# Sliding-window attention and a two-layer FFN on one core: five blocks' attention first, casts on GpSimd in load order, two output banks in every tile, column sums late

## The chip, the core and the metric

The kernel runs on one core of a Trainium2 chip. A core has a matrix engine (PE, which multiplies a stationary 128x128 operand with a moving one and writes its results to PSUM), a vector engine (DVE), an activation engine (ACT), GpSimd (POOL) and a sync engine (SP), which here only issues transfers. Each engine works through its own list of instructions in order; they meet at semaphores. PSUM has eight banks of 128 x 512 float32. The time is device microseconds (us) from start to end of one execution.

## The reference

Eight batches of eight heads, 576 positions, 64 channels per head. Each position attends to the positions at most 32 away; the result, heads side by side, is a matrix x of 4608 x 512, which goes through an FFN with a squared relu.

```python
scores = scale * np.matmul(q, k.transpose(0, 1, 3, 2))      # scale = 1/8
scores = np.where(np.abs(pos[:, None] - pos[None, :]) <= 32, scores, -1e9)
attn = np.exp(scores - np.max(scores, axis=-1, keepdims=True))
attn = attn / (np.sum(attn, axis=-1, keepdims=True) + 1e-09)
x = heads side by side of np.matmul(attn, v)                # 4608 x 512
h = x @ w_in                                                # 512 -> 2048
g = s * np.maximum(h, 0.0) ** 2 + b                         # s, b scalars
out = g @ w_out                                             # 2048 -> 512
```

The scalars are moved out of the second product: out = s * (r*r @ w_out) + b * (column sums of w_out). The last term is one vector, CVEC, spread over 128 partitions; it has to be there before the first output row can be finished.

## The kernel before

The 4608 rows are 36 blocks of 128. Attention works block by block (`attend(j)`), the FFN by tiles (`TILES`: eight of one block, then fourteen of two).

**Attention of a block.** q and k are loaded as float32 and cast to bf16 (`cast_q`, `cast_k`, line 471 through the helper `move`), turned on PE (`k_turn`, `q_turn`; bank TP) and copied to SBUF as kqt. A load can come in rows of 2 KB, eight positions each (`rows8`), which needs `turn_rows8` (line 528, 16 small matmuls), or in 256-byte pieces, one per head and position, with `turn_plain` (line 542, four). Scores (line 582) go to two banks, SC. DVE masks them and takes the extreme (line 598), ACT exponentiates and sums (line 606), DVE takes the reciprocal (line 617), and eight scalings of 128x128 (line 472) make P: on any of three engines for the first `NDIV` = 4 blocks, on GpSimd for the rest. P is turned on PE in the bank PTP for the first `PDMA` = 4 blocks (line 640), by a DMA transpose from block 4 on (line 633), and lands as PTS. The product with v (line 662) goes to the bank AV, and DVE copies it to XT, the FFN's input. Block 0 is worked in two halves (`FINE`), its second half in the banks HT1 and OUTP. From block 4 on, v's copy `vo` with halves swapped is made too (`make_vo`).

**FFN of a tile.** The first product (line 752) fills HT banks of 512 columns: for a tile of one block, 16 matmuls of 128 columns each, four such groups, one per quarter i0 to i3 of w_in. ACT takes the relu (line 761), DVE squares it into GT (line 780). The second product (line 803) takes 16 matmuls of 512 columns per block, in four groups of four, one per quarter o0 to o3 of w_out, into OUTP, or OUTP and PTP in turn after the first `NSOLO` = 2 blocks. DVE adds CVEC and writes the output tile (line 812), SP stores it. The last three tiles may use four banks.

**Weights.** w_in and w_out come as eight quarters of 1 MB (`load_w`) through four staging slots, which lie in a part of GT that tile 4 is the first to need. Each quarter is cast in four pieces, w_in's on GpSimd, w_out's on ACT or GpSimd.

**Column sums.** `cvec` multiplies a matrix of ones with all of w_out, four groups of four 512-column matmuls in OUTP (line 688), then scales on DVE (line 694). Output groups that use OUTP come behind it.

**The order.** Nothing is scheduled at run time. `_Plan` collects all steps with their data, an assumed cost and a key, and works out each engine's list once, when the kernel is built: at every step the engine that can go first takes its ready step with the lowest key. Wherever the plan sees PE idle over 300 ns at the start, it puts in filler matmuls (`fill`, lines 395 and 398), into banks that hold nothing yet. `FIRST` is the order of the first loads on SP's queue; the number of bars in it is the number of blocks whose attention is written ahead of the first tile's FFN. Steps on one bank are bound to the order in which they are written.

## Time and profile before

| | |
|---|---|
| Time, median of 3 runs | 329.05 us (328.51 to 329.32) |
| The profiled execution: time, span | 328.95 us, 327.2 us |
| PE, DVE, ACT, GpSimd busy | 96%, 71%, 65%, 56% of the span |
| First product, line 752, into ht and tp | 115.4 + 33.2 us busy on PE |
| Second product, line 803, into outp and ptp | 72.2 + 61.6 us busy on PE |
| DMA | 61.75 MB, 189 GB/s; packets under 512 B: 163820 of 173949 |
| Weight quarter, issue to landing | 11.4 us (w_in), 11.7 us (w_out), queueing included |

Busy time of PE overlaps between neighbouring matmuls, so a group's length from start to start is shorter than the duration that a line of the timeline shows. In a timeline, a line gives the start, the length of the group, the engine, the source line, the operation, what is written and read, and in brackets the idle time before it with what ended it. In a table by stretches, each engine's busy time is followed by its number of instructions; the last three columns are the granted clock of PE, the busy share of DMA and its GB/s. SPq is the sync engine issuing a transfer. A line "x16" of the first product is one group of 16 matmuls.

### The profile page before, as it was taken

To read this page: it belongs to the slowest core of one execution; us is meant where nothing else is said; L and a number is where in the kernel's file an instruction comes from. 1 tells how busy PE (TensorE), PEld (TensorE's weight loads), DVE (VectorE), ACT (ScalarE), POOL (GpSimd) and SP (SyncE) were. 2 spreads that over 40 slices of the span, in tenths; PEclk is the share of its full clock that TensorE was granted. 3 is DMA by queue.
4 is the path that set the end of the run, shared out by engine and by line. 5 is a ranking of instruction groups with operands and counts; after the bars stand their busy time and mean duration, and the time that the engine had idled before them with its cause. 6 is when DMAs were issued, how large, how long until landed. Compare 5 with 4: busy or idle time off the path is not lost.

```text
span 327.2 us, 10194 instructions
## 1 busy us (share of the span) xinstructions
PE 312.7 (96%) x3821; PEld 212.5 (65%) x3821; DVE 232.8 (71%) x988; ACT 214.0 (65%) x753; POOL 182.5 (56%) x394
## 2 busy tenths in 40 slices
PE   6675999999999999999999999999999999999996
PEld 4554776567767666766666666666666666666664
DVE  3459988879888878878787777777777677442432
ACT  3563896668769887867766666667777876533330
POOL 2537474897657988766655668486667453300000
PEclk9999999999999999999999999999999999999999
DMA  5999999999999999999999999999994332120011
GB/s 125 310 326 330 355 232 195 236 235 210 202 213 205 213 215 200 238 216 216 237 244 181 209 224 239 210 190 238 210 228 117 91 78 73 47 64 34 32 59 71
DMA packets 173949, 61.75 MB, mean 189 GB/s; under 512 B 163820, under 2 KB 164076, under 8 KB 173900
## 3 DMA queue, kind: packets, MB, share of 16 engines
q1 hardware_dynamic: 173612, 61.10, 88.3%
q8 instruction: 30, 0.49, 0.6%
q14 instruction: 19, 0.16, 0.2%
q10 hardware_dynamic: 288, 0.00, 0.0%
HBM read 36.70 MB, written 9.44 MB: 141 GB/s over the span
## 4 chain that ended last, share of the span: by engine, by line
PE 81%; DMA 7%; DVE 5%; SPq 4%; ACT 2%; issue 0%
PE ht L752 27%; PE outp L803 17%; PE ptp L803 16%; PE tp L752 9%; DMA q<-in_q_dram 4%; PE av L662 4%; PE sc L582 3%; DMA v<-in_v_dram 3%; PE sc L803 2%; ACT p L606 2%; PE av L803 2%; SPq L421 2%; DVE gt L780 1%; SPq L447 1%; SPq L450 1%; DVE kqn L471 1%
## 5 line engine op out<-in xcount | busy, mean ns | idle before, releaser
L472 POOL TENSOR_SCALAR p<-p,rc 128x128 bf16<-128x128 bf16 x257 | 101.8, 415 | 52.9 <-DVE rc L617 52.9
L606 ACT ACTIVATE p<-ss,mx 128x128 bf16<-128x128 f32 x288 | 111.8, 391 | 23.2 <-DVE mx L598 21.4
L752 PE MATMUL ht<-xt,win 128*128 128x256 bf16 (+1 forms) x1152 | 115.4, 249 | 0.6 <-POOL win L471 0.4
L752 PEld LDWEIGHTS ht<-xt,win 128*128 128x128 bf16 x1152 | 91.0, 98 | 23.7 <-POOL win L471 0.6
L780 DVE TENSOR_TENSOR gt<-r 128x512 bf16<-128x512 bf16 x144 | 68.5, 477 | 43.0 <-ACT r L761 42.2
L761 ACT ACTIVATE r<-ht 128x512 bf16<-128x512 f32 x112 | 66.3, 593 | 43.9 <-PE ht L752 40.3
L598 DVE CUSTOM_DVE_ANT_0 ss<-sc,mask 128x128 f32<-128x128 f32 x288 | 66.1, 282 | 18.0 <-PE sc L582 17.9
L803 PE MATMUL outp<-wout,gt 128*128 128x512 bf16 (+1 forms) x288 | 72.2, 374 | 0.0
L803 PE MATMUL ptp<-wout,gt 128*128 128x512 bf16 x240 | 61.6, 380 | 0.0
L606 ACT ACTIVATION_READ_ACCUMULATOR p<-ss,mx 128x1 f32 x288 | 54.4, 189 | 0.0
L471 POOL CAST ve<-v 128x512 bf16<-128x512 f32 x37 | 24.9, 672 | 29.1 <-PE av L662 16.6
L803 PEld LDWEIGHTS outp<-wout,gt 128*128 128x128 bf16 x288 | 26.1, 98 | 18.2
L803 PEld LDWEIGHTS ptp<-wout,gt 128*128 128x128 bf16 x240 | 22.3, 98 | 17.2
L752 PE MATMUL tp<-xt,win 128*128 128x256 bf16 x256 | 33.2, 273 | 0.0
L761 ACT ACTIVATE r<-tp 128x512 bf16<-128x512 f32 x32 | 18.9, 591 | 21.8 <-PE tp L752 20.6
L752 PEld LDWEIGHTS tp<-xt,win 128*128 128x128 bf16 x256 | 24.6, 98 | 8.8
L471 DVE CAST vo<-v 64x512 bf16<-64x512 f32 x54 | 27.1, 503 | 2.6 <-DMA v<-in_v_dram 1.8
L471 DVE CAST xt<-av 128x512 bf16<-128x512 f32 x35 | 24.0, 687 | 3.6 <-PE av L662 2.8
L598 DVE DVE_READ_ACCUMULATOR2_ANT mx<- 128x1 f32 x288 | 23.2, 81 | 0.0
L471 POOL CAST kqn<-q 128x512 bf16<-128x512 f32 x30 | 20.2, 672 | 2.9 <-DMA q<-in_q_dram 2.7
L471 POOL CAST kqn<-k 128x512 bf16<-128x512 f32 x31 | 19.0, 614 | 4.6 <-DMA k<-in_k_dram 4.5
L582 PEld LDWEIGHTS sc<-kqt 64*64 64x64 bf16 x864 | 12.1, 108 | 9.4 <-issue 6.5
(68 smaller groups left out, 228.4 us busy)
## 6 DMA issues: line engine op xcount, KB each, us to landing
out_dram<-outs SPq DMA_DIRECT2D x35, 256.0 KB, 3.4
q<-in_q_dram SPq DMA_DIRECT2D x32, 256.0 KB, 4.8
k<-in_k_dram SPq DMA_DIRECT2D x28, 256.0 KB, 4.8
v<-in_v_dram SPq DMA_DIRECT2D x28, 256.0 KB, 4.9
gt<-in_moe_w_in_dram SPq DMA_DIRECT2D x4, 1024.0 KB, 11.4
gt<-in_moe_w_out_dram SPq DMA_DIRECT2D x4, 1024.0 KB, 11.7
k<-in_k_dram SPq DMA_DIRECT2D x8, 192.0 KB, 3.8
v<-in_v_dram SPq DMA_DIRECT2D x8, 192.0 KB, 3.8
```

The costliest lines, as they stand in the source:

```text
L421: lastload[0] = add("sp", lambda e: [e.dma_start(w32, src)], 500, -LEAD - 900, writes=[("W32", s_, g) for g in range(4)], dsem=f"dw{s_}", ...
L447: return [e.dma_start(dst[r:r + n, :], src[b, :, s0:s0 + n, :].rearrange("h (c r) d -> c h (r d)", r=8)) for (b, s0, r, n) in pcs]
L471: return e.tensor_copy(dst, src)
L472: return e.tensor_scalar(dst, src, scale, 1.0, ALU.mult, ALU.mult)
L582: r = e.matmul(SC[hh][64 * u:64 * u + 64, pr, x0:x1], lhsT=KQT[kb][64 * hh:64 * hh + 64, NPAIR + pr, 64 * u:64 * u + 64], rhs=KQT[kt][64 * ...
L598: lambda e, ss=ss, x=x, y=y, pr=pr, hh=hh: e.tensor_tensor_reduce(out=SS[ss][:, x, :], in0=SC[hh][:, pr, :], in1=MASK[kind][:, :], scale=- ...
L606: lambda e, ss=ss, x=x, y=y: e.activation(P[pb][:, y, :], SS[ss][:, x, :], AF.Exp, bias=MX[mb][:, y:y + 1], scale=-1.0, accum_out=SM[mb][: ...
L662: r = e.matmul(avp[64 * hh:64 * hh + 64, pr, 64 * u:64 * u + 64], lhsT=vt[k0:k1, d0:d0 + 64], rhs=PTS[ptb][k0:k1, 2 * pr + hh, 64 * u:64 * ...
L752: r = e.matmul(hbank[:, nt * f:nt * f + nt], lhsT=WIN[:, kc, 128 * ft:128 * ft + 128], rhs=XT[:, kc, x0:x0 + nt], start=(kc == 0), stop=(k ...
L761: return e.activation(R1[rb][:, :], hbank[:, :], AF.Relu, bias=0.0, scale=1.0)
L780: return e.tensor_tensor(d, r, r, ALU.mult)
L803: r = e.matmul(op_[:, 0:cn], lhsT=GT[:, g_, fc, :], rhs=WOUT[:, fc, c0:c0 + cn], start=(fc == 0), stop=(fc == 15))
```

## The change

- `FIRST`: q1, k2, v2 go ahead of i0; i0 and i1, i2 and i3, and all of o0 to o3 follow each other. Five bars instead of three.
- All weight casts are GpSimd's, and all q and k casts from q1 and k2 on. Casts of the first loads get keys in the order of `FIRST` (`ckey`).
- k0 and q4 are no longer loaded in rows of 2 KB but in 256-byte pieces (`KROWS`, `QROWS`).
- P is turned in AV's bank (for the second half of block 0 in PTP's, where its product with v goes too), so that PTP is free for the second product: `NSOLO` is gone, and OUTP and PTP take turns from the first tile on.
- The column sums are written behind the second product of tile 0. 16 matmuls with 32 columns of ones put four partial sums into four strips of 32 partitions of TP; ACT copies them as bf16 (CHI), DVE writes the remainder (CLO), and two matmuls with a matrix of 1/32 (PART) add the strips; DVE scales to CVEC.
- Three assumed DMA times are raised by 170 or 150.

```diff
-    FIRST = "k0 q0 k1 v0 v1 i0 q1 k2 v2 i1 i2 q2 k3 v3 i3 o0 q3 k4 v4 o1 o2 o3|||"
+    FIRST = "k0 q0 k1 v0 v1 q1 k2 v2 i0 i1 q2 k3 v3 i2 i3 q3 k4 v4 o0 o1 o2 o3|||||"
-    WSET = {"i": ("pool",), "o": ("act", "pool")}
+    WSET = {"i": ("pool",), "o": ("pool",)}
-    ROWS8, NDIV = 5, 4
+    CKEY = 200
+    QROWS, KROWS, NDIV = range(0, 4), range(1, 5), 4
...
     def CSET(j):
-        return ANY if j < 6 else ("pool",)
+        return ("act", "dve") if j < 1 else ("pool",)
...
+        place = {x: i for i, x in enumerate(FIRST.replace("|", " ").split())}
+        def ckey(what, j, key):
+            return -9000 + 10 * place[what + str(j)] if what + str(j) in place else key
...
-                              dtime=2680, behind=lastload[0], ndesc=512)
+                              dtime=2850, behind=lastload[0], ndesc=512)
...
-                ptp, pres, avp, ares = PTP, "PTP", AV, "AV"
+                avp, ares = AV, "AV"
                 if fine and part:
-                    ptp, pres = halves(HT[1]), ("HT", 1)
-                    avp, ares = OUTP[:, :].rearrange("p (a b) -> p a b", b=128), ("OUTP", 0)
+                    avp, ares = PTPF[:, :].rearrange("p (a b) -> p a b", b=128), "PTP"
+                ptp = halves(PTPF if fine and part else AVF)
...
         def cvec():
-            for c in range(4):
-                def fn(e, c=c):
-                    for fc in range(4 * c, 4 * c + 4):
-                        r = e.matmul(OUTP[:, :], lhsT=ONES[:, 0:128], rhs=WOUT[:, fc, :],
-                                     start=(fc == 0), stop=(fc == 15))
-                    return r
-                add("pe", fn, 872, -300 + c, ...)
-            add("dve", lambda e: e.tensor_scalar(CVEC[:, :], OUTP[:, :], SCB[:, 1:2], None,
-                                                 ALU.mult), 750, -300, ...)
+            def quarters(e):
+                for i in range(4):
+                    for c in range(4):
+                        r = e.matmul(TPF[32 * c:32 * c + 32, :], lhsT=ONES[:, 0:32],
+                                     rhs=WOUT[:, 4 * c + i, :], start=(i == 0), stop=(i == 3))
+                return r
+            add("pe", quarters, 1000, CKEY, ...)
+            add("act", lambda e: e.copy(CHI[:, :], TPF[:, :]), 620, CKEY - 1000, ...)
+            add("dve", lambda e: e.tensor_tensor(CLO[:, :], TPF[:, :], CHI[:, :], ALU.subtract), 690, ...)
+            def total(e):
+                e.matmul(TPF[:, :], lhsT=PART[:, :], rhs=CHI[:, :], start=True, stop=False)
+                return e.matmul(TPF[:, :], lhsT=PART[:, :], rhs=CLO[:, :], start=False, stop=True)
+            add("pe", total, 440, CKEY - 1000, ...)
+            add("dve", lambda e: e.tensor_scalar(CVEC[:, :], TPF[:, :], SCB[:, 1:2], None,
+                                                 ALU.mult), 750, CKEY - 1000, ...)
...
-                                 )[0 if ocnt[0] < NSOLO else ocnt[0] % (4 if last else 2)]
+                                 )[ocnt[0] % (4 if last else 2)]
...
+                        if m == 0:
+                            n.tag = "full" if pt == 3 else "sums"
+                    if not cvec_done[0]:
+                        cvec()
+                        cvec_done[0] = True
```

More of the change, by code (lines that the diff above doesn't have):

```diff
@@ L328, in bass_sliding_window_symmetric__then__act_starrelu_kernel @@
         CVEC = sb((128, DM), F32, "cvec")
+        CHI, CLO = (sb((128, DM), BF16, nm) for nm in ("chi", "clo"))
+        PART = sb((128, 128), BF16, "part")
         SCB = sb((128, 2), F32, "scb")
@@ L356, in bass_sliding_window_symmetric__then__act_starrelu_kernel @@
         add("dve", lambda e: e.memset(NIL[:], 0.0), 100, K0, writes=["NIL"])
+        add("dve", lambda e: e.memset(PART[:], 1.0 / 32.0), 150, K0 + 90, writes=["PART"])
         add("dve", lambda e: e.memset(ZERO[:], 0.0), 150, K0, writes=["ZERO"])
@@ L426, in load_w @@
                 name = ("WIN", c, g) if which == "i" else ("WOUT", 4 * c + g)
[L427 to L428 removed]
+                cast(WSET[which], w32[:, g, :], ("W32", s_, g), dst, name, ckey(which, c, 0) + g)
         def parts(t0):
@@ L643, in attend @@
                     turned[j] = add("pe", turn, 59 * (c1 - c0), key + 4,
-                        reads=[("P", pb, y) for y in range(c0, c1)] + ["IDENT"], writes=[pres])
+                        reads=[("P", pb, y) for y in range(c0, c1)] + ["IDENT"], writes=[ares])
                     move(("act", "dve"),
                          {"act": 190.0 + 0.83 * 128 * (c1 - c0), "dve": 50 + 95.0 * (c1 - c0)},
-                         PTS[ptb][:, c0:c1, :], ptp[:, c0:c1, :], key + 4, [pres],
+                         PTS[ptb][:, c0:c1, :], ptp[:, c0:c1, :], key + 4, [ares],
                          [("PTS", ptb, y) for y in range(c0, c1)])
@@ L684, in cvec @@
         def cvec():
-            for c in range(4):
-                def fn(e, c=c):
-                    for fc in range(4 * c, 4 * c + 4):
-                        r = e.matmul(OUTP[:, :], lhsT=ONES[:, 0:128], rhs=WOUT[:, fc, :],
-                                     start=(fc == 0), stop=(fc == 15))
-                    return r
-                add("pe", fn, 872, -300 + c, reads=["ONES"] + [("WOUT", f) for f in range(4 * c, 4 * c + 4)],
-                    writes=[("OUTP", 0)]).tag = "full" if c == 3 else "sums"
-            add("dve", lambda e: e.tensor_scalar(CVEC[:, :], OUTP[:, :], SCB[:, 1:2], None,
-                                                 ALU.mult), 750, -300,
-                reads=[("OUTP", 0), "SCB"], writes=["CVEC"])
+            def quarters(e):
[4 more added lines that the diff above has]
+                return r
+            add("pe", quarters, 1000, CKEY, reads=["ONES"] + [("WOUT", f) for f in range(16)],
+                writes=["TP"])
+            add("act", lambda e: e.copy(CHI[:, :], TPF[:, :]), 620, CKEY - 1000, reads=["TP"],
+                writes=["CHI"])
+            add("dve", lambda e: e.tensor_tensor(CLO[:, :], TPF[:, :], CHI[:, :], ALU.subtract), 690,
+                CKEY - 1000, reads=["TP", "CHI"], writes=["CLO"])
+            def total(e):
+                e.matmul(TPF[:, :], lhsT=PART[:, :], rhs=CHI[:, :], start=True, stop=False)
+                return e.matmul(TPF[:, :], lhsT=PART[:, :], rhs=CLO[:, :], start=False, stop=True)
+            add("pe", total, 440, CKEY - 1000, reads=["PART", "CHI", "CLO"], writes=["TP"])
+            add("dve", lambda e: e.tensor_scalar(CVEC[:, :], TPF[:, :], SCB[:, 1:2], None,
+                                                 ALU.mult), 750, CKEY - 1000,
+                reads=["TP", "SCB"], writes=["CVEC"])
         done = [0]
```

41 lines of the change are left out of this document (18 added, 23 removed).

## The prediction

> **What bounds the kernel now.** I read the page first (engine totals, then the forty slices), then a table of busy time by stretch, then the instructions in order of time on each engine from 0 to 125 us, then the DMA queue's own order.
>
> ```profile
> PE 312.7 (96%) x3821; PEld 212.5 (65%) x3821; DVE 232.8 (71%) x988; ACT 214.0 (65%) x753; POOL 182.5 (56%) x394
> PE   6675999999999999999999999999999999999996
> PEclk9999999999999999999999999999999999999999
> DMA  5999999999999999999999999999994332120011
> ```
>
> PE is nearly full from the fifth slice (33 us) to the end, at full clock. So the change can gain only in front, where PE waits or idles on filler matmuls, and only if later PE work needs nothing that still comes too late. The front, by stretches (second column: PE's busy time):
>
> ```profile
> 20.00:25.00 5.00, 3.14 (x41) 2.37 (x39) 2.17 (x14) 4.05 (x18) 3.21 (x7) 1.00 1.14 276
> 25.00:30.00 5.00, 2.52 (x53) 1.98 (x53) 4.93 (x13) 1.95 (x4) 3.81 (x6) 1.00 1.06 382
> 60.00:70.00 10.00, 9.51 (x103) 5.12 (x101) 7.37 (x38) 7.48 (x33) 8.57 (x23) 1.00 1.09 252
> 70.00:80.00 10.00, 10.00 (x187) 7.68 (x186) 8.96 (x45) 7.42 (x27) 8.39 (x18) 1.00 1.27 210
> ```
>
> DMA is full throughout while the weights come. The second place where all FFN work hangs on one thing is around 70 us. In PE's order of time:
>
> ```profile
> 69.00 0.32 PE L662 MATMUL av<-pts,ve 128*64 128x64 bf16 x8
> 69.15 0.29 PE L662 MATMUL av<-pts,vo 128*64 128x64 bf16 x8
> 69.38 1.04 PE L803 MATMUL outp<-wout,gt 128*128 128x512 bf16 x4
> 70.34 0.45 PE L582 MATMUL sc<-kqt 64*64 64x128 bf16 x24
> 70.96 1.03 PE L803 MATMUL ptp<-wout,gt 128*128 128x512 bf16 x4
> 71.82 1.95 PE L752 MATMUL ht<-xt,win 128*128 128x128 bf16 x32
> 74.08 1.04 PE L803 MATMUL ptp<-wout,gt 128*128 128x512 bf16 x4
> ```
>
> At 71.82 tile 4's first product starts. Its input is block 4's attention: the av at 69.00, and the copy to xt on DVE from 69.49 to 70.18. Counting back, 16 first-product groups (x16, 0.89 us each) and 15 of 16 output groups (x4, 0.87 us from start to start) of tiles 0 to 3 are done by then; the sixteenth comes at 74.08. So "all of tiles 0 to 3, then tile 4" is reached at 71.82 + 0.87 = 72.7. Against this point I measure. Block 4's chain on GpSimd and the DMA queue:
>
> ```profile
> 58.97 2.96 POOL L472 TENSOR_SCALAR p<-p,rc 128x128 bf16<-128x128 bf16 x8
> 61.95 2.25 SPq L633 DMA_TRANSPOSE pts<-p  x1
> ```
>
> **The change, part by part.** Durations are from this execution: span 327.2, time 328.95, 0.1 under the median of 329.05.
>
> *Load order and casts.* Total bytes stay; the order moves. Casts that waited for a load show its landing: v1 10.1, i0 13.2, i1 19.7, i2 23.8, i3 28.4, o0 31.8, v4 35.5, o1 38.3, o2 40.7, o3 43.6. A weight thus takes 2.0 to 4.1, a q, k, v triple 2.6 to 3.7. k0 becomes 256-byte pieces: between nothing and 1.04 (the step from k1 to v0, which loads so); I take 0.35, the nearer end, as k1's 2 KB-row load took 0.9 itself. After: v2 13.3, i0 16.8, i1 20, i2 26.5, i3 29.2, o0 36, o1 38.7, o2 41.3, o3 44. On GpSimd a weight's four casts take 2.3 to 2.7: i0 ready 19.4, i1 22.3, i2 29, i3 31.9, o0 38.5, o1 41.2, o2 43.8, o3 46.5, then k5 and q4 (now 256-byte pieces too, nothing to 0.5 more) by 47.7. Ten casts leave DVE and ACT for GpSimd (q1 to q3, k2 to k4, four of w_out); between i0 and o3 it has about 38 casts of 0.65, 25 us in 29.
>
> *Attention.* Block 0's scores stay at 11.0. Its DVE stretch loses two casts, one of which waited 1.0 for q1, so block 1's scores move from 18.9 to 16. Block 1's P was held to 30.3 by DVE, which stood in its queue for q2 (2.83 idle at 24.39); that cast is GpSimd's now, and P can be turned at 23. Block 2's scores follow at 26.5 instead of 30.8. Turning P in AV's bank adds a wait for the xt copy before; that copy (26.6 for block 1, 41.6 for block 2) is ahead of the next turn (37 and 44.7), so nothing. PTS copies stay 0.7 to 1.0.
>
> *FFN.* Its first group now waits for i0's cast (19.6) instead of xt (20.57 before). The eight groups of tiles 0 and 1 then follow i2 and i3 and end at 37.1. PE has little but two fillers from 26.7 to 29: an idle of about 2.3, where the longest now (2.48 at 26.06) left the clock at 1.00. ACT's exponentials of block 2 queue behind the relu of the group that waits for i2, to 33.2; P is scaled by 36.7 and turned at 37.1, block 3's scores are at 37.7.
>
> *Output banks and late column sums.* In the new order the output groups of tiles 0 and 1 alternate in two banks as soon as o0 is cast: seven stand ahead of block 4's scores. The kernel before has two there, since the sums (4 x 0.87) and eight zero fillers (1.05) hold OUTP until 47. With waits for o1 and o2 of 0.3 to 0.5 I get to block 4's scores ending at 50.3 (51.8 before). The sums become 16 matmuls of 32 columns in four column strips. If strips run beside each other that is four matmuls of 0.217, about 1.0; if not, sixteen, 3.5. The nearest row is the av: eight 64-wide matmuls into two column halves are issued within 0.15 (69.00 to 69.15), where 512 columns one after the other take 0.217; I take 1.0, the end that it is nearer to. The Trainium skill, "TensorE: Matmul & The Clock Gate", Part 3, gives three such strips a speedup of 2.38; by that the sums would be an estimated 1.5 or less.
>
> *From 50.3 to tile 4.* Ahead of block 4's av stand sums 1.0, five first-product groups 4.5, nine output groups 7.8, the two closing matmuls 0.43, two scores 0.76, six turns of 0.23: 15.9, so PE is there at 66.2 with nothing of tiles 0 to 3 left. Block 4's own chain: its sum of exponentials stands on DVE behind CVEC and two output writes. The closing matmuls start at 53.9, after two tile groups and the copies CHI (ACT 0.6) and CLO (DVE 0.7); CVEC 0.74 ends at 55.1, a square 0.45 and two output writes of 0.75 end at 57.1, sum, a copy and reciprocal at 58.0, GpSimd's eight scalings (2.96) at 61, the DMA issue (2.25) at 63.2. SP's queue ahead of it holds two output stores, four loads: issued by 60. Block 5's transpose was usable at most 3.85 after its issue (69.85 to 73.70), so the av is at 67.1 and xt 1.2 later: tile 4 at 68.4. I add 0.9 because DVE squares and scalings beside GpSimd's casts take up to twice as long (0.87 against 0.41; seven scalings in 2.38 against six in 1.07), which falls on two or three steps of this chain. So 69.3: gain 72.7 - 69.3 = 3.4.
>
> *After it.* The av of blocks 5 to 8 come 6.1, 5.1, 5.5 and 8 apart in the new order; before, 4.7, 5.8, 8.4 and 7.3, with scores and loads well ahead. The third could wait; its scores are at 69 instead of 70.3, its transpose at about 85 against 86 needed. I cost it at nothing, bounds -0.5 and +1. The tail's banks are as before.
>
> Sum: 328.95 - 3.4 = 325.6.
>
> A rule against the change: the Trainium skill, "SBUF — State Buffer", section "Who interferes with whom", says GpSimd shares a port pair with DVE and that one fully blocks the other for some DVE forms. The trace agrees: the squares and scalings above, and single GpSimd casts of 0.80 to 1.44 where most take 0.61. What that would make of the time is the first rival.
>
> **The rivals.**
> *GpSimd becomes the bound of the front (slower).* All casts now stand in one queue in load order. From i0's landing at 16.8, 38 casts of 0.65 would be over by 41.5, so loads, not casts, set the 46.5. At 0.87 each (what several v casts between 35 and 58 took) they end at 49.9: k5 and q4, block 4's scores, scalings and transpose move by 3.4 and the gain is gone. It decides from that mean; at 0.90 tile 4 is at 73.8 and the time 330.1, at 0.95 it is 332. For it: DVE is 90 to 100% busy in most of 25 to 50, when GpSimd now casts most. Against: with contention present, k casts average 0.614, q and v 0.672. I put it at 330.1.
> *Strips not beside each other.* +2.5 on the sums, CVEC, block 4's scalings and tile 4: gain 0.9, 328.1. The scores' 24 matmuls in 0.38 speak against it.
> *The transpose's landing is set by the DMA queue, not by its issue.* DMA is 80 to 100% full from 44 on and as many bytes stand ahead of block 4's transpose as before (17 loads and two stores against 18 and one). Then the av stays at 69.0, tile 4 starts at 70.25 with nothing owed: 326.5.
> *Block 4 is not late at all.* If DVE is free sooner, PE's own 66.2 counts, tile 4 at 67: gain 5.7, 323.3.
>
> **How the numbers follow.** Forecast 0.44, queue-bound transpose 0.13, block 4 early 0.12, serial strips 0.09, GpSimd bound 0.22. About 0.3% (1 us) is what a measurement here can tell. The serial case lies about at its edge and is counted as no change, 0.01 of the others with it; the GpSimd case is slower, the rest faster: faster 0.68, same 0.10, slower 0.22. Leaving out the best half of the early case and half of the slow one gives 323.2 to 330.3; the forecast's own range is 324.3 to 327.
>
> **What would show it.** In the changed kernel: first P turn of block 1 near 23 and block 4's scores near 50; seven output groups ahead of them; sums of some 1 us; block 4's av at 67 to 69, with a PE wait of 1 to 2 us there that did not exist; tile 4 at 68 to 70. It is wrong if GpSimd's casts end after 48, if DVE's wait for CVEC holds block 4's scalings beyond 63, or if PE waits again for the av of blocks 6 to 9.

## The result, and the profile after

The changed kernel takes 338.59 us (median, 337.88 to 340.18); the kernel before, beside it, 328.87 us. The ratio is 1.0302 (95% interval 1.0261 to 1.0342): slower by 9.7 us, where 325.6 was forecast and 330.3 was the upper end. The profiled execution is of 338.28 us with a span of 336.0; its span is 8.8 us over that of before, and I account for these.

The engine totals and the forty slices of the changed kernel:

```profile
PE 309.4 (92%) x3756; PEld 213.2 (63%) x3802; DVE 228.3 (68%) x956; ACT 224.5 (67%) x775; POOL 190.0 (57%) x407
PE   7758789969799799999999999999899999999996
PEclk9999999998999999999999999999999999999999
```

PE's share falls from 96% to 92%. The row has holes where that of before had nines: slices five and six (34 to 50 us), then nine, eleven and fourteen (67 to 76, 84 to 92 and 109 to 118 us), and one at 235 to 244. What is lost up to tile 4 is counted below as tile 4's late start. No engine has become the bound.

PE's busy time in three stretches (second column; third from the end the granted clock), first in the kernel before, where all are full, then in the changed kernel:

```profile
70.00:80.00 10.00, 10.00 (x187) 7.68 (x186) 8.96 (x45) 7.42 (x27) 8.39 (x18) 1.00 1.27 210
80.00:90.00 10.00, 10.00 (x147) 7.35 (x146) 8.95 (x34) 7.87 (x33) 7.01 (x15) 1.00 1.17 208
110.00:120.00 10.00, 10.00 (x139) 6.85 (x140) 8.41 (x32) 8.47 (x34) 9.14 (x20) 1.00 0.93 199
```
```profile
70.00:80.00 10.00, 7.38 (x138) 6.63 (x128) 7.80 (x43) 7.58 (x32) 7.81 (x19) 0.83 1.15 239
80.00:90.00 10.00, 8.06 (x147) 5.62 (x148) 8.58 (x31) 6.41 (x25) 6.41 (x16) 1.00 1.17 176
110.00:120.00 10.00, 7.74 (x112) 5.38 (x112) 8.05 (x43) 9.24 (x39) 8.83 (x22) 1.00 1.09 231
```

PE in order of time, changed kernel, just ahead of tile 4 and at two later places, and DVE's copy that ends the first wait (`...` marks lines left out):

```profile
69.74 0.45 PE L588 MATMUL sc<-kqt 64*64 64x128 bf16 x24
70.12 0.40 PE L548 MATMUL tp<-ident,kqn 128*128 128x128 bf16 x4
72.68 0.40 PE L548 MATMUL tp<-ident,kqn 128*128 128x128 bf16 x4 [2.16 <-DVE kqt L477]
73.00 0.32 PE L668 MATMUL av<-pts,ve 128*64 128x64 bf16 x8
...
74.88 4.06 PE L768 MATMUL ht<-xt,win 128*128 128x128 bf16 x48 [0.32 <-DVE xt L477]
...
88.20 0.40 PE L548 MATMUL tp<-ident,kqn 128*128 128x128 bf16 x4 [1.72 <-DVE kqt L477]
...
113.56 1.92 PE L768 MATMUL ht<-xt,win 128*128 128x256 bf16 x16 [1.33 <-DVE xt L477]
```
```profile
72.20 0.42 DVE L477 COPY kqt<-tp 128x512 bf16<-128x512 bf16 x1
```

Tile 4's first product starts at 74.88, with nothing of tiles 0 to 3 owed: 2.2 us behind the 72.7 of before, where 3.4 ahead was forecast. By 70.5 PE has done all of tiles 0 to 3; it is out of FFN work. The next step in its list, a turn for a later block, needs bank TP, which a DVE copy (kqt) empties from 72.20 on, after the eight readings of block 6's scores (70.52 to 72.28). Block 4's av stands behind that turn, although its P has landed by 68.9 (3.3 us after the issue began). From there the loss adds up: 1.2 us because the clock drops to half behind the idle time (48 matmuls of tile 4 take 4.06 us where 32 at full clock take 1.95); 1.72 at 88.20; 1.33 at 113.56 and 0.77 at 116.25 (for ACT's relu); 1.28 at 241.76 (xt). With the 2.2 that is 8.5 of the 8.8.

What the new parts do by themselves can be read there too. The column sums, and GpSimd, DVE and the sync engine around block 4 and the casts; the last line is six scalings in the kernel before:

```profile
54.24 0.45 PE L588 MATMUL sc<-kqt 64*64 64x128 bf16 x24
54.62 1.05 PE L694 MATMUL tp<-wout,ones 128*32 128x512 bf16 x16
```
```profile
37.60 9.57 POOL L477 CAST wout<-gt 128x512 bf16<-128x512 f32 x16
61.90 3.62 POOL L478 TENSOR_SCALAR p<-p,rc 128x128 bf16<-128x128 bf16 x8 [4.30 <-DVE rc L623]
37.33 3.16 DVE L478 TENSOR_SCALAR p<-p,rc 128x128 bf16<-128x128 bf16 x6
65.55 1.35 SPq L639 DMA_TRANSPOSE pts<-p  x1
37.03 1.07 DVE L472 TENSOR_SCALAR p<-p,rc 128x128 bf16<-128x128 bf16 x6
```

The sums take 1.05 (1.0 was forecast). The sixteen casts of w_out stand back to back, at 0.60 each: GpSimd is full from 37 to 48 and hardly slowed (three of the sixteen took 0.80). DVE is slowed: six scalings of block 2 take 3.16, where six took 1.07 in the kernel before. Block 4's scores come at 54.24 (forecast to end at 50.3), its scalings end at 65.5 (61), and the transpose is issued at 66.9 (63.2).

### The profile page after: what moved, and what is told of

Same layout as the page of the kernel before. It is cut to its first block, busy times and chain, and to the rows that moved or that the text cites. A ratio compares the mean times of both kernels' runs of the same rounds, so it can differ in the third digit from the quotient of the medians.

```text
span 336.0 us, 10129 instructions
## 1 busy us (share of the span) xinstructions
PE 309.4 (92%) x3756; PEld 213.2 (63%) x3802; DVE 228.3 (68%) x956; ACT 224.5 (67%) x775; POOL 190.0 (57%) x407
## 4 chain that ended last, share of the span: by engine, by line
PE 76%; DVE 8%; SPq 7%; ACT 4%; DMA 3%; issue 2%
PE ht L768 25%; PE ptp L816 16%; PE outp L816 15%; PE tp L768 9%; SPq L453 4%; PE av L668 3%; ACT p L612 3%; PE sc L588 3%; DMA v<-in_v_dram 3%; SPq L428 2%; PE sc L816 2%; PE av L816 2%; DVE p L478 1%; DVE outs L830 1%; DVE vo L477 1%
## 5 line engine op out<-in xcount | busy, mean ns | idle before, releaser
L796 DVE TENSOR_TENSOR gt<-r 128x512 bf16<-128x512 bf16 x144 | 70.0, 491 | 53.3 <-ACT r L777 52.5
L816 PE MATMUL outp<-wout,gt 128*128 128x512 bf16 (+1 forms) x250 | 63.7, 373 | 2.2 <-issue 1.1
L477 POOL CAST ve<-v 128x512 bf16<-128x512 f32 x37 | 23.6, 638 | 40.1 <-PE av L668 31.1
L816 PEld LDWEIGHTS ptp<-wout,gt 128*128 128x128 bf16 x256 | 24.1, 98 | 23.7 <-issue 0.4
L816 PEld LDWEIGHTS outp<-wout,gt 128*128 128x128 bf16 x272 | 24.3, 98 | 19.8
L477 DVE CAST xt<-av 128x512 bf16<-128x512 f32 (+1 forms) x36 | 24.5, 681 | 11.9 <-PE av L668 11.6
L477 POOL CAST kqn<-k 128x512 bf16<-128x512 f32 x35 | 23.5, 672 | 2.6 <-DMA k<-in_k_dram 2.6
L477 POOL CAST kqn<-q 128x512 bf16<-128x512 f32 x35 | 23.9, 682 | 1.2 <-DMA q<-in_q_dram 0.7
L482 ACT CAST vo<-v 64x512 bf16<-64x512 f32 x34 | 20.9, 614 | 3.6 <-PE av L668 3.0
L477 DVE CAST vo<-v 64x512 bf16<-64x512 f32 x30 | 19.6, 653 | 2.6 <-DMA v<-in_v_dram 2.3
```

What stands on the lines that cost most here:

```text
L477: return e.tensor_copy(dst, src)
L482: return e.copy(dst, src)
L796: return e.tensor_tensor(d, r, r, ALU.mult)
L816: r = e.matmul(op_[:, 0:cn], lhsT=GT[:, g_, fc, :], rhs=WOUT[:, fc, c0:c0 + cn], start=(fc == 0), stop=(fc == 15))
```

## The experiments

The change has parts of two kinds: output banks, late sums and five bars on the one hand, loads and casts (with the times that the plan assumes for the loads) on the other. The variants below set parts back to what they were. The same statement has other line numbers in each variant, and `...` in an edit marks lines left out that only carry the same part (`WKEY`, the choice of engine in `cast_k`). Ratios are to runs of the kernel before on the same chip; differences between medians of two variants can come from two chips, so where the ratios give another size, both are named.

### The two halves apart

`e2_loads_only` is the kernel before with the loads and casts of the change; `e3_banks_sums_only` is the changed kernel with all of that set back (the edit of e2 against the kernel before is the same the other way round, with three bars).

```diff
--- the changed kernel
+++ e3_banks_sums_only
-    FIRST = "k0 q0 k1 v0 v1 q1 k2 v2 i0 i1 q2 k3 v3 i2 i3 q3 k4 v4 o0 o1 o2 o3|||||"
+    FIRST = "k0 q0 k1 v0 v1 i0 q1 k2 v2 i1 i2 q2 k3 v3 i3 o0 q3 k4 v4 o1 o2 o3|||||"
-    WSET = {"i": ("pool",), "o": ("pool",)}
+    WSET = {"i": ("pool",), "o": ("act", "pool")}
-        return ("act", "dve") if j < 1 else ("pool",)
+        return ANY if j < 6 else ("pool",)
...
-            return -9000 + 10 * place[what + str(j)] if what + str(j) in place else key
+            return WKEY[what] + 4 * j if what in "io" else key
-    QROWS, KROWS, NDIV = range(0, 4), range(1, 5), 4
+    QROWS, KROWS, NDIV = range(0, 5), range(0, 5), 4
-                              dtime=2850, behind=lastload[0], ndesc=512)
+                              dtime=2680, behind=lastload[0], ndesc=512)
-                              ndma=len(pcs), dtime=(850.0 if rows8 else 1400.0) * tot / 128,
+                              ndma=len(pcs), dtime=(700.0 if rows8 else 1250.0) * tot / 128,
```

> The kernel before with the new load order, k0 and q4 in 256-byte pieces, all casts as in the changed kernel, and nothing else: three bars, P in PTP, early sums in OUTP, one output bank for the first two blocks. Theory 1 (later weights, and GpSimd's casts of w_out beside DVE's scalings, set the loss): block 2's scalings take about 3 us on DVE as in the changed kernel, the first output group starts after 46, tile 4 starts at 74 or later, time 334 to 340. Theory 2 (the new banks and late sums set it: more output groups ahead of the scores of blocks 4 and 5, and CVEC and two output writes ahead of block 4's scalings on DVE): near the kernel before, 326 to 331, tile 4 at 70 to 73.

Measured: 334.45 us, ratio 1.0146 (1.0124 to 1.0167), in the range of theory 1; tile 4 starts at 73.5.

> The changed kernel with load order, rows, cast engines, cast keys and assumed DMA times of before; banks, late sums and five bars stay. Theory 1: block 2's scalings on DVE are short again (about 1 us), tile 4 starts before 70 with all of tiles 0 to 3 done, time 323 to 328. Theory 2: block 5's scores stay behind 62 and its av behind 79, PE waits on DVE between 70 and 120 stay, time 333 to 340.

Measured: 329.02 us, ratio 0.9977 (0.9955 to 0.9998), between the ranges of the two theories. Tile 4, with everything of tiles 0 to 3 done, starts 3.1 us ahead of the 72.7 of before. PE of this variant, with two later waits and the start of tile 13, and after it the start of tile 13 in the kernel before:

```profile
67.95 0.32 PE L670 MATMUL av<-pts,ve 128*64 128x64 bf16 x8 [0.33 <-DMA pts<-p]
69.57 1.07 PE L770 MATMUL ht<-xt,win 128*128 128x128 bf16 x16 [1.18 <-DVE xt L479]
...
105.62 1.05 PE L770 MATMUL ht<-xt,win 128*128 128x256 bf16 x8 [1.07 <-DVE xt L479]
...
110.66 0.32 PE L670 MATMUL av<-pts,ve 128*64 128x64 bf16 x8 [0.78 <-DMA pts<-p]
...
179.60 1.04 PE L770 MATMUL ht<-xt,win 128*128 128x256 bf16 x8
```
```profile
179.61 1.04 PE L752 MATMUL ht<-xt,win 128*128 128x256 bf16 x8
```

So the loss lies with loads and casts: alone 5 us, on top of the other half 9.6. And the gain forecast for the other half is there at 69.6 but not at the end. The two late waits take 1.85 of the 3.1. Another 0.84 was never gained: at its tile 4, e3 still owes the scores of one block (0.38) and two turns (0.46) that the kernel before has done by then; 0.4 stays unaccounted for. At tile 13 both have done the same scores, av products and 65 output groups, and stand at 179.6: in the profiled executions (329.08 and 328.95 us) nothing of the gain is left. The ratio's 0.2% is less than the 0.3% that the prediction takes as the least that a measurement here can tell.

### Casts on all engines again, and three bars

```diff
--- the changed kernel
+++ e4_casts_shared
-    WSET = {"i": ("pool",), "o": ("pool",)}
+    WSET = {"i": ("pool",), "o": ("act", "pool")}
-        return ("act", "dve") if j < 1 else ("pool",)
+        return ANY if j < 6 else ("pool",)
...
--- the changed kernel
+++ e5_three_bars
-    FIRST = "k0 q0 k1 v0 v1 q1 k2 v2 i0 i1 q2 k3 v3 i2 i3 q3 k4 v4 o0 o1 o2 o3|||||"
+    FIRST = "k0 q0 k1 v0 v1 q1 k2 v2 i0 i1 q2 k3 v3 i2 i3 q3 k4 v4 o0 o1 o2 o3|||"
```

> The changed kernel, load order kept, but casts may go where they could before (q and k of the first blocks on ACT, DVE or GpSimd; w_out on ACT or GpSimd). If GpSimd alone as the place of the casts costs the time: block 4's scores before 52 instead of 54.2, time 3 us or more below the changed kernel (335 or less). If it is the order of loads or the banks: within 2 us of 338.6.

Measured: 336.33 us, ratio 1.0201 (1.0184 to 1.0218), between the two ranges.

> The changed kernel with three bars, so only three blocks' attention is written ahead of the first FFN tile. Both theories: bars change little in themselves, 335 to 341; a time below 333 would say that the written order of attention and FFN is the cause.

Measured: 343.57 us, ratio 1.0417 (1.0393 to 1.0441), more than expected. The five bars are no part of the loss: without them 5 us more are lost. Sharing the casts gives back 2.3 us, a third of the loss by the ratios, so GpSimd's queue is not the main cause.

### Order, casts, and what holds the attention back

`e7_new_order` and `e8_casts_pool` add one part each to e3. `e9_pdma6` and `e10_ndiv6` ask of e3 why its gain goes: the first turns P of blocks 4 and 5 on PE, the second lets three engines scale it.

```diff
--- e3_banks_sums_only
+++ e7_new_order
-    FIRST = "k0 q0 k1 v0 v1 i0 q1 k2 v2 i1 i2 q2 k3 v3 i3 o0 q3 k4 v4 o1 o2 o3|||||"
+    FIRST = "k0 q0 k1 v0 v1 q1 k2 v2 i0 i1 q2 k3 v3 i2 i3 q3 k4 v4 o0 o1 o2 o3|||||"
--- e3_banks_sums_only
+++ e8_casts_pool
-    WSET = {"i": ("pool",), "o": ("act", "pool")}
+    WSET = {"i": ("pool",), "o": ("pool",)}
-        return ANY if j < 6 else ("pool",)
+        return ("act", "dve") if j < 1 else ("pool",)
...
-            return WKEY[what] + 4 * j if what in "io" else key
+            return -9000 + 10 * place[what + str(j)] if what + str(j) in place else key
--- e3_banks_sums_only
+++ e9_pdma6
-    PDMA, KQDMA, AHEAD, GATE = 4, 11, 4, 6
+    PDMA, KQDMA, AHEAD, GATE = 6, 11, 4, 6
--- e3_banks_sums_only
+++ e10_ndiv6
-    QROWS, KROWS, NDIV = range(0, 5), range(0, 5), 4
+    QROWS, KROWS, NDIV = range(0, 5), range(0, 5), 6
```

> The kernel with only the new banks and the late column sums (329.02 us, tile 4 at 69.6), plus the new order of the loads; the casts keep the engines and the order that they had before. The loads part as a whole costs 9.6 us on top of that kernel. Theory A, the order itself starves the first products (weights i0 to i3 land 2 to 3.5 us later, and the later q, k, v no earlier in what counts): most of it, 333 to 338, and tile 4 at 72 to 75. Theory B, GpSimd's queue with all casts in load order is the cost: 328 to 331, tile 4 at 68.5 to 71.

Measured: 329.00 us, ratio 0.9971 (0.9945 to 0.9997), tile 4 at 70.0. Theory A fell: the order alone costs nothing.

> The kernel with only the new banks and the late column sums, plus all casts on GpSimd in the order of the loads; the loads keep their order of before. Theory A (the order of the loads is the cost): 328.5 to 331.5, tile 4 at 69 to 71. Theory B (GpSimd's queue is the cost, and what DVE loses beside it): 333 to 338, scalings of P on DVE at 0.5 each instead of 0.18, tile 4 at 72 to 75.

Measured: 331.97 us, ratio 1.0073 (1.0047 to 1.0099), tile 4 at 72.4. Theory B's direction, not its size.

> The kernel with only the new banks and the late column sums reaches tile 4 at 69.6, 3.1 us sooner than before, and loses that again by 120 us, where PE waits for the attention of blocks 4 to 10. Here P of blocks 4 and 5 is turned on PE (8 small matmuls and a copy) instead of by a DMA. If a full DMA queue's transposes hold the attention back: tile 4 at 66 to 68.5, and 326 to 328.5 in all. If the loads of q, k, v themselves or GpSimd's scalings hold it: tile 4 about 69, and 329 to 330.5, since PE gets about 1 us more work.

Measured: 330.60 us, ratio 1.0035 (1.0013 to 1.0057). Block 4's av comes at 66.0, 1.9 us sooner than in e3, and tile 4 starts at 68.3 with one output group owed; so the transpose does hold block 4. But at 106 PE waits 1.49 for a later block's transpose and 0.92 for DVE, and the total is no better.

> The same kernel (new banks, late column sums, all else as before); the scalings of P of blocks 4 and 5 may go to ACT, DVE and GpSimd instead of GpSimd alone (2.96 us of eight in a row there). If GpSimd's scalings hold blocks 4 and 5 back: tile 4 1 to 2 us sooner, at 67.5 to 68.5, and 327 to 328.7 in all. If the transposes' place in the DMA queue sets the landing: no change within 0.3, 328.5 to 329.5.

Measured: 329.49 us, ratio 1.0018 (0.9983 to 1.0053), tile 4 at 68.9. Here block 4's scalings are done at 59.4 instead of 62.7, 3.3 us sooner. Its transpose, of e3 and then of e10, on the sync engine:

```profile
62.72 3.18 SPq L641 DMA_TRANSPOSE pts<-p  x1
```
```profile
61.03 1.10 SPq L458 DMA_DIRECT2D v<-in_v_dram  x1
62.24 2.83 SPq L641 DMA_TRANSPOSE pts<-p  x1
```

3.3 us in the scalings become 0.5 at the issue and 0.55 at the av (67.40 against 67.95): the transpose now stands behind a load in the sync engine's list, its issue lasts 2.8 to 3.2, and it lands 5.1 to 5.2 after the issue began in both. So GpSimd's scalings are worth half a us there, and what the sync engine issues ahead of the transpose holds block 4 next. That is the prediction's third rival in kind, not in size: it had the av at 69.0.

### The cast's place in the plan, or pieces and assumed times

In e3 the order costs nothing and casts on GpSimd cost 3 us; all of it together costs 9.6. Two things were left: that casts of first loads go before all other work of their engine (`ckey`), and the small edits, pieces of k0 and q4 and the three assumed DMA times.

```diff
--- the changed kernel
+++ f1_old_keys
-            return -9000 + 10 * place[what + str(j)] if what + str(j) in place else key
+            return WKEY[what] + 4 * j if what in "io" else key
--- the changed kernel
+++ f2_old_rows_times
-    QROWS, KROWS, NDIV = range(0, 4), range(1, 5), 4
+    QROWS, KROWS, NDIV = range(0, 5), range(0, 5), 4
-                              dtime=2850, behind=lastload[0], ndesc=512)
+                              dtime=2680, behind=lastload[0], ndesc=512)
-                              ndma=len(pcs), dtime=(850.0 if rows8 else 1400.0) * tot / 128,
+                              ndma=len(pcs), dtime=(700.0 if rows8 else 1250.0) * tot / 128,
--- e7_new_order
+++ f3_order_keys
-            return WKEY[what] + 4 * j if what in "io" else key
+            return -9000 + 10 * place[what + str(j)] if what + str(j) in place else key
--- e7_new_order
+++ f4_order_rows_times
-    QROWS, KROWS, NDIV = range(0, 5), range(0, 5), 4
+    QROWS, KROWS, NDIV = range(0, 4), range(1, 5), 4
-                              dtime=2680, behind=lastload[0], ndesc=512)
+                              dtime=2850, behind=lastload[0], ndesc=512)
-                              ndma=len(pcs), dtime=(700.0 if rows8 else 1250.0) * tot / 128,
+                              ndma=len(pcs), dtime=(850.0 if rows8 else 1400.0) * tot / 128,
```

> The changed kernel (338.6 us) with one thing back: the casts stand in the planner's order by the due times of before, not by the order of the loads; they stay on GpSimd. So far: the new order of the loads alone costs nothing (329.0), all casts on GpSimd in load order cost 3 (332.0), the load order of casts on shared engines with the new load times and pieces gave 336.3. If it is the place of the casts ahead of all other work of their engine that costs: 329 to 333. If the new pieces and load times cost: 336 to 339.

Measured: 336.38 us, ratio 1.0200 (1.0174 to 1.0226).

> The changed kernel with k0 and q4 in the pieces of before and the planner's load times of before. If the casts' place costs: 335 to 339. If pieces and load times cost (k0 in 256-byte pieces delays block 0, or the longer times in the plan turn the order of PE's work round): 329 to 333.

Measured: 329.13 us, ratio 0.9977 (0.9955 to 0.9999), tile 4 at 70.6.

> New banks, late column sums, new order of the loads (329.0 so far), plus the casts in load order on all three engines; pieces and load times of before. If the casts' place costs: 333 to 337, with waits for casts in DVE's and ACT's queues. If pieces and load times cost: 328.5 to 331.

Measured: 330.53 us, ratio 1.0026 (1.0008 to 1.0044).

> New banks, late column sums, new order of the loads, plus the new pieces and load times; casts by the engines and due times of before. If the casts' place costs: 328.5 to 331. If pieces and load times cost: 333 to 337.

Measured: 333.79 us, ratio 1.0118 (1.0086 to 1.0150).

All four agree: banks, late sums, five bars, new load order, casts on GpSimd and their keys together cost nothing (f2). The pieces and the assumed times cost 9.5 us there, and 4.8 on top of e7 (f4). What casts on GpSimd cost (e8) hangs on what stands beside them: in the new order and with the old times they cost nothing (f2 against e7).

### Pieces or assumed times

An assumed DMA time is part of no instruction. The plan uses it once, when it writes each engine's list. With the order, the list settles two more things: which engine takes a step that several may take, and how many fillers there are. The changed kernel has 92 fillers and ACT makes 34 of the 64 copies `vo`; g5, with the times set back, has 85 and 23.

```diff
--- the changed kernel
+++ g5_times_back
-                              dtime=2850, behind=lastload[0], ndesc=512)
+                              dtime=2680, behind=lastload[0], ndesc=512)
-                              ndma=len(pcs), dtime=(850.0 if rows8 else 1400.0) * tot / 128,
+                              ndma=len(pcs), dtime=(700.0 if rows8 else 1250.0) * tot / 128,
--- the changed kernel
+++ g1_load_times_back
-                              ndma=len(pcs), dtime=(850.0 if rows8 else 1400.0) * tot / 128,
+                              ndma=len(pcs), dtime=(700.0 if rows8 else 1250.0) * tot / 128,
--- the changed kernel
+++ g2_weight_time_back
-                              dtime=2850, behind=lastload[0], ndesc=512)
+                              dtime=2680, behind=lastload[0], ndesc=512)
--- the kernel before
+++ g4_before_load_times
-                              ndma=len(pcs), dtime=(700.0 if rows8 else 1250.0) * tot / 128,
+                              ndma=len(pcs), dtime=(850.0 if rows8 else 1400.0) * tot / 128,
```

> The changed kernel (338.6) with only the planner's assumed load times set back (2850 to 2680 for a weight, 1400 to 1250 and 850 to 700 for a q, k or v block); no operation of the chip changes, only the order of instructions. If the assumed times cost: 328.5 to 331. If the smaller pieces of k0 and q4 cost: 335 to 339.

Measured: 331.68 us, ratio 1.0036 (1.0004 to 1.0069). Three numbers in the plan are worth 6.9 us (8.7 by the ratios). The rest, 331.68 against f2's 329.13, is the pieces, and the landings are later with them. GpSimd's casts of i2, i3 and the last w_out quarter, in f2 and then in g5:

```profile
25.80 2.48 POOL L477 CAST win<-gt 128x512 bf16<-128x512 f32 x4 [0.38 <-DMA gt<-in_moe_w_in_dram]
29.73 2.29 POOL L477 CAST win<-gt 128x512 bf16<-128x512 f32 x4 [1.46 <-DMA gt<-in_moe_w_in_dram]
43.78 2.29 POOL L477 CAST wout<-gt 128x512 bf16<-128x512 f32 x4 [0.38 <-DMA gt<-in_moe_w_out_dram]
```
```profile
27.25 2.30 POOL L477 CAST win<-gt 128x512 bf16<-128x512 f32 x4 [1.13 <-DMA gt<-in_moe_w_in_dram]
31.37 2.48 POOL L477 CAST win<-gt 128x512 bf16<-128x512 f32 x4 [1.82 <-DMA gt<-in_moe_w_in_dram]
45.69 2.29 POOL L477 CAST wout<-gt 128x512 bf16<-128x512 f32 x4 [0.67 <-DMA gt<-in_moe_w_out_dram]
```

Each waited for its landing: 1.45, 1.64 and 1.91 later, with only k0 ahead of them in other pieces. In the nine kernels of this study with the new order and k0 in 256-byte pieces the sync engine was through with issuing the last weight at 34.0 to 35.0; in the four with the same order and rows of 2 KB at 32.4 to 34.0. Why the lag grows from 0.6 at i0 to 1.9 these runs do not tell. One of the four, h2, differs from f2 only in the place of the sums and yet casts i2 and i3 at 26.93 and 31.08, so not all of the lag is due to the pieces. Nor do the runs part the landings from the lists: the edit also raises what the plan assumes for k0 and q4 (700 to 1250), so g5's lists differ from f2's.

> The changed kernel with only the times of q, k, v loads set back (1400 to 1250, 850 to 700). In the plan a block of 128 positions then takes 3 x 1.25 + 2 x 1.6 + 0.7 = 7.65 us of transfers instead of 8.1, against some 7.4 us of PE work per block in the trace of before; if that pace, with attention put ever later into PE's list, is the cause: 328.5 to 332, no PE wait for kqt after 75 us. If the weights' time is: 334 to 339.

Measured: 331.93 us, ratio 1.0046 (1.0023 to 1.0069).

> The changed kernel with only the weights' time set back (2850 to 2680). If the pace of the q, k, v loads in the plan is the cause: 335 to 339. If the weights' time is: 329 to 332.

Measured: 334.85 us, ratio 1.0139 (1.0099 to 1.0180). The times of q, k and v cost 3.2 us with the weights' time as before and 6.7 with it raised; the weights' time 0.2 and 3.7. They don't add up, as changes in a list don't.

> The kernel before (329.05) with only the times of q, k, v loads raised in the plan, as the change has them (1250 to 1400, 700 to 850); nothing else differs but the order of instructions. If the pace in the plan is the cause: 333 to 339, with PE idle after 70 us. If it costs only together with the other parts: 328.5 to 331.

Measured: 329.93 us, ratio 1.0003 (0.9983 to 1.0023). In the kernel before the same two numbers cost nothing, though the av of blocks 4 to 7 come later there too, at 70.9, 76.0, 83.5 and 89.8 instead of 69.0, 73.7, 79.5 and 87.9. My pace argument in g1's expectation would have made it slow, so the pace alone is not it.

### Why the numbers cost only here

`g6_banks_load_times` is e3 with just the q, k and v times raised; `h2_sums_early` is f2 with the column sums ahead of block 4.

```diff
--- e3_banks_sums_only
+++ g6_banks_load_times
-                              ndma=len(pcs), dtime=(700.0 if rows8 else 1250.0) * tot / 128,
+                              ndma=len(pcs), dtime=(850.0 if rows8 else 1400.0) * tot / 128,
--- f2_old_rows_times
+++ h2_sums_early
-    CKEY = 200
+    CKEY = -200
```

> New banks and late column sums only (329.02), plus the raised q, k, v load times in the plan (1250 to 1400, 700 to 850). In the kernel before, these times cost nothing (329.9). If they cost where PE has no FFN work left over ahead of block 4, as in the changed kernel: 333 to 337, with further PE waits between 70 and 125 us. If they cost only beside the new load order and GpSimd's casts: 328.5 to 331.

Measured: 333.49 us, ratio 1.0103 (1.0055 to 1.0150), 4.5 over e3. Neither the load order nor GpSimd's casts are needed for it. This pair shows the mechanism best, since nothing else differs. The transpose of block 5 on the sync engine, and PE around it, in e3 and then in g6:

```profile
69.47 1.55 SPq L641 DMA_TRANSPOSE pts<-p  x1
69.57 1.07 PE L770 MATMUL ht<-xt,win 128*128 128x128 bf16 x16 [1.18 <-DVE xt L479]
70.69 1.95 PE L770 MATMUL ht<-xt,win 128*128 128x128 bf16 x32
74.17 0.32 PE L670 MATMUL av<-pts,ve 128*64 128x64 bf16 x8
```
```profile
69.22 1.30 SPq L641 DMA_TRANSPOSE pts<-p  x1
69.06 0.40 PE L550 MATMUL tp<-ident,kqn 128*128 128x128 bf16 x4 [1.31 <-DVE kqt L479]
71.09 1.07 PE L770 MATMUL ht<-xt,win 128*128 128x128 bf16 x16 [1.63 <-DVE xt L479]
72.90 3.33 PE L770 MATMUL ht<-xt,win 128*128 128x128 bf16 x32
78.78 0.32 PE L670 MATMUL av<-pts,ve 128*64 128x64 bf16 x8
```

The transpose is issued no later in g6 and lands no later (73.3, e3: 73.6), and no wait stands before the av at 78.78, 5.4 us after the landing. The av is 4.6 us later because of what the list has ahead of it. A second turn ahead of tile 4 waits for DVE (1.31), and then xt is waited for (1.63): tile 4 starts 1.5 later. The half clock follows and costs 1.4 (32 matmuls in 3.33 instead of 1.95). And two output groups, which e3 does behind this av, are now ahead of it: 1.7. That fits a plan that reckons with longer loads, expects a later landing and fills the time; the plan's own reckoning was not printed.

Why not in the kernel before? Its av of blocks 4 to 7 come at 69.0, 73.7, 79.5 and 87.9, e3's at 68.0, 74.2, 79.2 and 87.1: the two banks and the late sums let PE finish tiles 0 to 3 sooner, and attention is no quicker. When block 4's av comes, the kernel before has done 13 of the 16 output groups of tiles 0 to 3, and with the raised times 14; e3 and g6 have done all 16. So in the kernel before PE has work whenever an av is late: 10.00 of 10 in each stretch from 70 to 120, and with the raised times in all of them but the one from 100 to 110 (9.19). In e3 nothing is owed at 69.57, and from there on an av that comes late can leave PE idle. That the missing backlog is the reason is argued from these two pairs (g4 against before, g6 against e3); no run gave the backlog back alone. The changed kernel shows the same on a larger scale: block 4's av at 73.00 and block 5's at 82.41, 9.4 apart, where e3 has 6.2.

> The changed kernel with old pieces and old load times (329.13), and the column sums ahead of block 4's scores instead of behind them. There block 4's sum of exponentials stood behind CVEC and two output writes on DVE (58.5), its scalings ended at 63.0, its transpose was issued at 63.1 to 65.1, its av came at 68.55 and tile 4 at 70.56. If CVEC's place on DVE holds block 4: scalings done 1 to 2 us sooner, tile 4 at 68.5 to 70, 327.5 to 329 in all. If it is PE's own list or the DMA queue: tile 4 at 70 to 71.5 and 328.8 to 330.5.

Measured: 330.05 us, ratio 1.0000 (0.9976 to 1.0024). The edit moved little: the sums stayed at 51.8, only block 4's scores changed places with them. Scalings ended 0.4 sooner (62.7), the transpose was issued 0.5 later (63.6), the av came at 69.2. So CVEC's place is not shown to matter, nor excluded. No variant beats the kernel before by more than 0.3%: the best are e7 (0.9971), e3 and f2 (0.9977).

The parts in a row, each line with one more than the line above. They do not add up independently: g4 and g6 show that a part's cost hangs on what is there already.

| kernel | adds | median, us | ratio |
|---|---|---|---|
| e3 | banks, late sums, five bars | 329.02 | 0.9977 |
| e7 | order of the loads | 329.00 | 0.9971 |
| f3 | casts' keys in that order | 330.53 | 1.0026 |
| f2 | all casts on GpSimd | 329.13 | 0.9977 |
| g5 | k0 and q4 in pieces, with the times that the plan assumes for pieces | 331.68 | 1.0036 |
| g1 | a weight's time 2850 | 331.93 | 1.0046 |
| the changed kernel | times of q, k, v 1400 and 850 | 338.59 | 1.0302 |

## Why the prediction was wrong

*The step that failed most was one that the sum does not have.* The diff raises three assumed DMA times. The prediction costs the order of loads, the casts, the banks and the sums, but not these; it took the lists as they came and worked out when each entry is ready. They are worth 6.9 of the 13.0 us between 325.6 and 338.59 (g5; 8.7 by the ratios). In the terms of the sum: the 15.9 us of PE work ahead of block 4's av were right (15.8, from 54.7 to 70.5). Wrong were their start, block 4's scores, which end 4.4 later than the forecast 50.3, and the wait of 2.16 for bank TP just ahead of the av, put at nothing: the P of block 4 had landed by 68.9, its av came at 73.00. Behind tile 4, g6 shows what the raised times alone do: block 5's av comes 5.4 us after its P has landed, with a turn and two output groups put ahead of it.

*k0 and q4 in pieces* were put at 0.35 for k0 and nothing to 0.5 for q4. They cost about 2.5 (f2 against g5; 1.9 by the ratios), with the change of the lists that goes with them. That term was mis-sized. k0 itself lands sooner in pieces (its cast starts at 4.33 in g5, at 5.88 in f2), but the weights behind it later. With the old pieces the forecast landings are near: i2 26.5 forecast, 25.8 in f2, 27.7 in the changed kernel; i3 29.2, 29.7, 31.9.

*"After it" at nothing, -0.5 to +1*, failed. e3 has most of the forecast gain at tile 4 and nothing of it at tile 13. The point measured against was itself too generous: "all of tiles 0 to 3, then tile 4" leaves out 0.84 of attention work that e3 does later. The reason given, scores and loads well ahead, looked at the wrong link: the av of blocks 5 to 8 came no sooner in e3 (74.2, 79.2, 87.1, 95.7) than before (73.7, 79.5, 87.9, 95.3), so PE, with tiles 0 to 3 done 3 us sooner, met them with nothing left to do.

*Block 4's chain and tile 4* came near where nothing else interferes, in part by luck. e3: scores at 50.3 (forecast: ending at 50.3), sums 1.05 (1.0), CVEC ended at 56.5 (55.1), scalings done at 62.7 (61), transpose issued by 65.9 (63.2), av at 67.95 (67.1), tile 4 at 69.57 (69.3). The issue ended 2.7 late, and 2.0 from there to the landing, where 3.85 was reckoned, made up for most of it. In f2 with the new load order tile 4 is at 70.6. In medians the miss of 13.0 is 6.9 for the times, 2.5 for the pieces and 3.5 for a forecast gain of which f2 (329.13) keeps nothing.

*The rivals.* GpSimd as the bound gave the right side, 330.1, by the wrong mechanism: casts stayed at 0.60 and below the 0.87 where it would decide, although k5 and q4 were cast by 48.3, just past the bound named; f2, with the same casts, is not slower. Only in the old load order do casts on GpSimd cost 3 us (e8), and why is open. Serial strips: excluded, 1.05. The transfer queue as the bound of block 4's transpose: e9 and e10 show that it matters in e3; in the changed kernel the transpose was issued as soon as the scalings were done (65.5), and its landing did not decide. Block 4 early: not seen. Two more signs came true: scalings beyond 63, at 65.5, and PE waiting again for the av of blocks 6 to 9, as for xt of block 9 at 113.56; the wait at 88.20 is for bank TP. Right were the seven output groups ahead of block 4's scores.

## What to carry to other kernels

Where an order is worked out at build time from assumed costs, a changed cost is a change of the program: compare the lists of the engines from end to end before pricing any operation, and look for products that moved behind other work although their input is ready at the same time, for steps that changed their engine, and for fillers. A gain at one point lasts only if the next supplier keeps up; before claiming it to the end, check what the bounding engine would do without its backlog. A transfer reordered or cut smaller is priced by the landings of all that stands behind it, not by its own.

## What the runs showed of the hardware

*The clock falls to half behind waits that small matmuls interrupt, and stays there for 3.4 us or a multiple of it.* PE of the changed kernel by microseconds (second column busy, third from the end the clock):

```profile
71.00:72.00 1.00, 0.00 (x0) 0.00 (x0) 1.00 (x13) 1.00 (x6) 1.00 (x4) 1.00 1.16 262
72.00:73.00 1.00, 0.32 (x4) 0.23 (x4) 0.62 (x5) 1.00 (x7) 0.99 (x2) 1.00 1.22 243
73.00:74.00 1.00, 0.85 (x43) 0.70 (x42) 0.42 (x1) 1.00 (x6) 0.41 (x1) 1.00 1.21 237
74.00:75.00 1.00, 0.68 (x11) 0.42 (x7) 0.94 (x4) 0.64 (x2) 0.20 (x1) 0.51 1.06 314
76.00:77.00 1.00, 1.00 (x13) 1.00 (x11) 1.00 (x11) 0.92 (x5) 1.00 (x4) 0.50 1.08 215
77.00:78.00 1.00, 1.00 (x17) 1.00 (x16) 0.68 (x2) 0.40 (x1) 1.00 (x3) 0.78 1.09 221
```

PE was idle for 2.16 us, with turns, av and scores around it. The clock went to half at 74.0, before the large matmuls began, and came back at 77.4. In g6 idles of 1.31 and 1.63 with 0.40 of work between them did the same (72.4 to 75.8), in g1 one of 1.79 (71.5 to 74.9). But in f2 one of 1.58 did not, nor, in the kernel before, one of 2.48. Longer stretches occur too: 6.8 us in e3 (17.2 to 24.0) and f2 (20.0 to 26.9), in the part where PE has fillers, and 10.2 in e5 (64.1 to 74.3). The Trainium skill, "TensorE: Matmul & The Clock Gate", gives the gate a free-running window of some 3.4 us. The lengths of the half-clock stretches agree, and so does it that the same gap may or may not cost, by where it falls. The share of busy time in a window tells more than one gap: in the 3.41 us ahead of the three drops PE was busy for 1.20, 1.67 and 1.62, and in the same window of f2, without a drop, for 1.84. Cut into such windows, the first 120 us of the twenty traces have 19 with PE busy for under 1.45 us, and the clock is at half behind each; from there to 1.9 it goes either way, and above that it is mostly full. The page's rule of thumb, no idle gaps of over some 3 us, is too mild here: 1.79 among small matmuls was enough.

*Four column strips pay almost in full.* In f2 the sixteen 32-column matmuls start at 51.82 and the next group at 52.80: 0.98, where sixteen of 512 columns one after the other would take 16 x 0.217 = 3.5. The speedup of 2.38 that the same page of the Trainium skill (Part 3) gives is for three strips; with four it comes to some 3.5 here.

*Beside GpSimd's casts, DVE loses more than GpSimd*: scalings of 0.18 became 0.53, while a run of sixteen casts stayed at 0.60 each.
